# Numbering all transfers in program order over both DMA queues, and storing the last block whole

## The chip, the cores and the metric

The kernel runs on one core of a Trainium2 chip. The metric is device time in microseconds (us). PE is the matrix engine (TensorE), DVE the vector engine, ACT the scalar engine, POOL GpSimd, and SP the sync engine, which computes nothing here and issues transfers. "SPq" and "ACTq" are the instruction queues of SP and ACT when they issue transfers (DMAs). A transfer is asynchronous: the engine issues it, goes on, and a completion semaphore is raised when the data has landed.

## What is computed

q, k and v are float32; S1, S2 and the weights are float64 and reach the device as raw 64-bit words; the output is float32. A sketched attention is followed by a multiplicative feed-forward network:

```python
def phi(x):                                   # 64 features per row
    a = einsum('rd,bhsd->bhsr', S1, x);  b = einsum('rd,bhsd->bhsr', S2, x)
    return (a[..., :, None] * b[..., None, :]).reshape(..., r * r)
q_p, k_p = phi(q), phi(k)                     # q, k, v: batch 4, heads 4, seq 1088, dim 32; r = 8
kv = einsum('bhsf,bhsd->bhfd', k_p, v);  z = k_p.sum(axis=2)
x = (q_p @ kv) / (q_p @ z + 1e-6)             # then to (4352 tokens, 128)
a, b = x @ w1, x @ w2                         # 128 -> 1024
out = ((a * b) @ w3) @ w_out                  # 1024 -> 1024 -> 128
```

## The kernel before

The program is made of some hundreds of named steps. A list written out by hand, `ORDER`, gives the one order in which they are recorded; each step issues its instructions on whichever engines it uses. A helper at the end of the kernel (lines 1544 to 1548) then ties every instruction to the one before it *on the same engine*, so that the scheduler keeps the written order engine by engine. Nothing ties an instruction of one engine to one of another, except data.

The tokens come in eight main groups, `g0` to `g7`, of 512 tokens (two for each batch), and one group `gr` of 256 tokens, the last 64 rows of each of the four batches. For each group the feed-forward part (function `ffn`) runs over eight chunks c of the hidden width: step `a` (line 1458) and step `b` (line 1468) are matmuls, step `c` copies one result out on ACT, step `m` multiplies on DVE, and step `o` (line 1481, for `gr` line 1488) accumulates the product with the folded w3 and w_out into the output bank. w3 and w_out are folded into one matrix earlier, so two matmul layers become one.

At the end of a main group, `g.oT` (line 1497) transposes the output bank into SBUF on DVE, and `g.st` stores it with four DMAs of 64 KB on SP (function `main_dst`, line 1435). These pieces are 128 bytes long at the output (32 floats). The last group `gr` is different. It has two output banks; `gr.oT0` copies bank 0 out on ACT and `gr.oT1` copies bank 1 out on DVE (both line 1508). The stores (function `rest_dst`, line 1441) have pieces of 512 bytes:

- `gr.st0` stores bank 0 whole, 64 KB, from ACT's queue;
- `gr.st1` stores the first half of bank 1, 32 KB, from SP's queue;
- `gr.st2` stores the second half of bank 1, 32 KB, from ACT's queue.

In `ORDER` the tail reads `... g7.oT ... g7.st ... gr.oT0 gr.oT1 gr.st2 gr.st1 gr.st0`, followed by idle matmuls (`warm`). So on SP the four DMAs of `g7.st` come before `gr.st1`, and on ACT `gr.st2` comes before `gr.st0`. Earlier stores on SP, in this order, are those of `g4`, `g5`, `g6`, `g1` and `g2`.

The framework gives the transfers eight completion semaphores in turn, numbered 0 to 7, in the order in which its scheduler takes them. A transfer waits, on the queue that issues it, until the transfer that had its semaphore before has landed. The issuing queue is in order, so everything behind a waiting transfer on that queue waits too. Which transfer gets which number follows from the order that the scheduler took across engines, which the chains of line 1544 leave open.

Loads of inputs and weights are on SP as well, except that the two large loads of the first k block (`k0.load0`, `k0.load1`, line 506) are on ACT. They and the last stores are the only transfers that ACT issues.

Of the kernel before, what the change touches and what calls it, by code (L numbers as in the profile page):

```python
# [112 lines left out]
g4.7o g7.1m g4.oT g6.5m gr.2b g7.4a g6.2b gr.2a g7.4c g7.7a gr.2c gr.2m gr.0b gr.6m g6.2m g7.4m gr.3c g4.st g5.st  # L113
g7.7c g6.0o g6.5o g6.2o g6.6o g6.4o g6.1o g6.3o g6.7o gr.0m g6.oT g7.7b g6.st g7.0o gr.0o0 g7.6o g7.5o gr.3b g1.st
gr.1b g7.4o g2.st g7.2o gr.1m g7.7m gr.3m g7.3o g7.1o g7.7o gr.0o1 gr.6o1 gr.6o0 gr.5o0 g7.oT gr.1o0 gr.5o1 gr.1o1
gr.4o1 gr.3o1 gr.2o1 g7.st gr.7o1 gr.4o0 gr.3o0 gr.2o0 gr.7o0 gr.oT0 gr.oT1 gr.st2 gr.st1 gr.st0 warm25 warm20 warm28
"""


# [4 lines left out]
def make_steps(ctx, tc, q, k, v, S1, S2, moe_w1, moe_w2, moe_w3, moe_w_out, out):  # L124
    nc = tc.nc
    dve, act, pe, pool, sp = nc.vector, nc.scalar, nc.tensor, nc.gpsimd, nc.sync
    B, H, S, D = q.shape
    r = S1.shape[0]
    DM, DF = moe_w1.shape
# [6 lines left out]
    NT = S // 32  # L136
# [6 lines left out]
    def step(name):  # L143
        def keep(f):
            assert name not in steps, name
            steps[name] = f
            return f
        return keep
# [13 lines left out]
    def sb(tag, shape, dtype=F32, bufs=1, name=None):  # L162
        return place(work, tag, shape, dtype, bufs, name or tag)

    def ps(tag, shape, name):
        return place(psum, tag, shape, F32, 1, name)
# [1270 lines left out]
                             oT[i * 32:(i + 1) * 32, :nT * 32].rearrange("p (T d) -> p T d", d=32))  # L1437
        return dst

    def rest_dst(oT, u, t0=0, n=32):  # L1440
        (sp if u and not t0 else act).dma_start(bass.AP(tensor=out.tensor, offset=(NT - 2 + u + t0 * NT) * DM,
                             ap=[[NT * DM, n], [S * DM, B], [1, DM]]), oT[t0 * B:(t0 + n) * B])

    ab_sb, o_ps = {}, {}

    def ffn(g, n, dst):
        for c in range(NC):
            halves = 2 if (g, c) in HALVES else 1
            w = n // halves
            for u in range(halves):  # L1450
                x = {}
                su = "" if halves == 1 else "ab"[u]
                c0 = u * w

                @step(f"g{g}.{c}{su}a")
                def _(c=c, c0=c0, x=x, w=w):
                    x["a"] = ps("h", [128, 512], "a_ps")
                    pe.matmul(x["a"][:, :w], w_of(0, c), xT[g][:, c0:c0 + w], start=True, stop=True)  # L1458

                @step(f"g{g}.{c}{su}c")  # L1460
                def _(x=x, w=w):
                    x["s"] = sb("ffa", [128, 512], bufs=2)
                    act.copy(x["s"][:, :w], x["a"][:, :w])  # L1463

                @step(f"g{g}.{c}{su}b")
                def _(c=c, c0=c0, x=x, w=w):
                    x["b"] = ps("h", [128, 512], "b_ps")
                    pe.matmul(x["b"][:, :w], w_of(1, c), xT[g][:, c0:c0 + w], start=True, stop=True)  # L1468

                @step(f"g{g}.{c}{su}m")  # L1470
                def _(c=c, c0=c0, x=x, u=u, w=w):
                    if u == 0:
                        ab_sb[g, c] = sb("ab", [128, 512])
                    dve.tensor_mul(ab_sb[g, c][:, c0:c0 + w], x["s"][:, :w], x["b"][:, :w])  # L1474

            if g != "r":
                @step(f"g{g}.{c}o")
                def _(c=c):
                    if c == 0:
                        o_ps[g] = ps("out", [128, 512], "ps_o")  # L1480
                    pe.matmul(o_ps[g], w3o[:, c], ab_sb[g, c], start=c == 0, stop=c == NC - 1)  # L1481
            else:
                for u in range(2):
                    @step(f"g{g}.{c}o{u}")
                    def _(c=c, u=u):
                        if c == 0:
                            o_ps[g, u] = ps(("out", "kvz")[u], [128, DM], "ps_or")
                        pe.matmul(o_ps[g, u], ab_sb[g, c][:, u * DM:(u + 1) * DM], w3o[:, c],  # L1488
                                  start=c == 0, stop=c == NC - 1)

        if g != "r":
            oT = {}

            @step(f"g{g}.oT")
            def _():
                oT[0] = sb("oT", [128, 512], bufs=2)
                dve.transpose(oT[0], o_ps[g])  # L1497

            step(f"g{g}.st")(lambda: dst(oT[0]))
        else:  # L1500
            z = {}
            for u in range(2):
                @step(f"g{g}.oT{u}")
                def _(u=u):
                    if u == 0:
                        z["o"] = sb("oT", [128, 512], bufs=2)
                    z[u] = z["o"][:, u * DM:(u + 1) * DM]
                    (dve.tensor_copy if u else act.copy)(z[u], o_ps[g, u])

                if u == 0:  # L1510
                    step(f"g{g}.st0")(lambda: dst(z[0], 0))
                else:
                    for i in range(2):
                        step(f"g{g}.st{1 + i}")(lambda i=i: dst(z[1], 1, 16 * i, 16))

    for g in range(8):
        b, half = divmod(g, 2)
        if g < 2:
            q_part(g, b, half * 512, 512, "AL"[g])
        elif b < 2:  # L1520
            q_wide(g, b, half * 512, 512, lambda t, g=g: (g, t * 128))
        elif half == 0:
            q_wide(g, b, 0, 1024, lambda t, g=g: (g + t // 2, t % 2 * 256))
        ffn(g, 512, main_dst(b, half * 16, 16))
    q_wide("r", None, 0, 256, lambda t: ("r", t))
    ffn("r", 256, rest_dst)

    for i, n in enumerate(WARM):
# [4 lines left out]
@with_exitstack  # L1533
def kernel(ctx: ExitStack, tc: tile.TileContext, *args: bass.AP):
    nc = tc.nc
    steps = make_steps(ctx, tc, *args)
    traced = nc.cur_bb.bb.instructions
    behind = mybir.DependencyInfo(mybir.DependencyClass.NoSync, mybir.DependencyReason.SCHED_ONLY)
    chained = [e.engine for e in (nc.vector, nc.scalar, nc.tensor, nc.gpsimd, nc.sync)]
    last, seen = {}, len(traced)  # L1540
    for name in ORDER.split():
        steps.pop(name)()
    assert not steps, sorted(steps)
    for ins in traced[seen:]:
        if ins.engine in chained:
            if ins.engine in last:
                tc.add_manual_dep(ins, last[ins.engine].name, behind, reason="order")
            last[ins.engine] = ins


# [28 lines left out]
```

## Time and profile before

| what | us |
|---|---|
| median of 3 runs | 256.16 (255.90 to 256.43) |
| the profiled execution, its own time | 255.97 |
| its span in the trace | 254.2 |
| PE busy in it | 245.7 (97%) |
| DVE, ACT, POOL busy | 159.2, 100.3, 82.3 |
| last matmul group of `gr` (line 1488) ends | 247.6 |
| last transfer issued (SP, line 1441) | 251.32 |

The span goes from the first to the last recorded event of the program; the own time of the execution includes what lies around it. The transfers by queue, the first thing that the page says of them, are these (queue and kind, packets, MB, share of the time of 16 DMA engines):

```profile
q1 hardware_dynamic: 30352, 21.02, 33.4%
q10 hardware_dynamic: 768, 0.62, 0.8%
```

q1 is SP's queue and q10 is ACT's. A row of the timeline reads: start in us, length in us, engine, line, operation, output and input, how many, and in brackets the idle time of the engine before it and what ended it. For a transfer the length is that of its issue, not of the data's way; the landing comes later.

### The profile page before, as it was taken

What the parts mean: (1) busy time and instruction counts of PE and PEld (TensorE: products, weight loads), DVE (VectorE), ACT (ScalarE), POOL (GpSimd) and SP (SyncE); (2) the same over time, 40 slices, a digit from 0 to 9 for tenths busy, and PEclk for the clock granted to TensorE, in tenths of its full rate; (3) what the DMA queues carried; (4) which work ended last, traced back from release to release, by engine and by line L of the source; (5) the groups of instructions that cost most, each with busy time, mean ns of one, the idle gap of its engine ahead of it and who ended that gap; (6) DMA issues with size and microseconds to landing.
All of it is one profiled execution on the core that took longest, in us unless ns stands there. A gap on an engine that the chain in (4) does not pass through costs nothing.

```text
span 254.2 us, 6032 instructions
## 1 busy us (share of the span) xinstructions
PE 245.7 (97%) x2511; PEld 140.1 (55%) x2511; DVE 159.2 (63%) x351; ACT 100.3 (39%) x186; POOL 82.3 (32%) x111
## 2 busy tenths in 40 slices
PE   8899999999999999999999999999999999999990
PEld 6789756456644657576454444444435544554570
DVE  4899898999999969647839584523073144531310
ACT  3757689865665675111522343123202200120000
POOL 3269469476273497983002340000000000000000
PEclk9999999999999999999999999999999999999997
DMA  5679856899599420030200000000020000022532
GB/s 184 182 208 361 251 139 155 228 232 235 144 276 232 92 83 0 3 92 1 41 3 3 0 0 5 0 0 3 0 41 0 3 0 0 0 46 37 83 54 52
DMA packets 31147, 22.02 MB, mean 87 GB/s; under 512 B 21264, under 2 KB 25616, under 8 KB 30992
## 3 DMA queue, kind: packets, MB, share of 16 engines
q1 hardware_dynamic: 30352, 21.02, 33.4%
q10 hardware_dynamic: 768, 0.62, 0.8%
q8 instruction: 20, 0.33, 0.6%
q14 instruction: 7, 0.06, 0.1%
HBM read 19.40 MB, written 2.23 MB: 85 GB/s over the span
## 4 chain that ended last, share of the span: by engine, by line
PE 87%; DVE 5%; DMA 2%; POOL 2%; issue 1%; SPq 1%; DVEq 0%; POOLq 0%
PE a_ps L1458 23%; PE b_ps L1468 23%; PE ps_o L1481 22%; PE ps_w3o L480 6%; PE ps_x L1417 2%; PE ps_g L608 2%; PE ps_ac L1303 2%; DMA qh<-in_q_dram 2%; PE ps_or L1488 1%; PE ps_kv L718 1%; POOL RC L345 1%; PE idle_ps L223 1%; PE ps_ab L676 1%; DVE k_m L182 1%; PE ps_kq L754 0%
## 5 line engine op out<-in xcount | busy, mean ns | idle before, releaser
L1474 DVE TENSOR_TENSOR ab<-ffa,b_ps 128x512 f32<-128x512 f32 (+1 forms) x74 | 45.9, 636 | 44.2 <-PE b_ps L1468 34.7
L1463 ACT COPY ffa<-a_ps 128x512 f32<-128x512 f32 (+1 forms) x74 | 38.6, 556 | 86.6 <-PE a_ps L1458 80.8
L1468 PE MATMUL b_ps<-xT,w 128*128 128x512 f32 (+1 forms) x148 | 67.4, 560 | 0.0
L1458 PE MATMUL a_ps<-xT,w 128*128 128x512 f32 (+1 forms) x148 | 66.8, 561 | 0.0
L1481 PE MATMUL ps_o<-ab,w3o 128*128 128x512 f32 x128 | 60.8, 595 | 0.0
L1468 PEld LDWEIGHTS b_ps<-xT,w 128*128 128x128 f32 x148 | 27.4, 190 | 27.9 <-issue 23.4
L1458 PEld LDWEIGHTS a_ps<-xT,w 128*128 128x128 f32 x148 | 27.1, 190 | 27.6 <-issue 22.1
L1481 PEld LDWEIGHTS ps_o<-ab,w3o 128*128 128x128 f32 x128 | 23.8, 190 | 26.0 <-issue 24.3
L444 POOL TENSOR_TENSOR w3c<-cv_c,cv_m 128x512 int32<-128x512 int32 x16 | 20.3, 1284 | 12.5 <-DVE cv_c L433 8.8
L1497 DVE STREAM_TRANSPOSE oT<-ps_o 128x512 f32<-128x512 f32 x8 | 5.7, 713 | 18.7 <-PE ps_o L1481 18.7
L480 PEld LDWEIGHTS ps_w3o<-wo,w3T 128*128 128x128 f32 x128 | 15.4, 192 | 2.9 <-issue 2.2
L480 PE MATMUL ps_w3o<-wo,w3T 128*128 128x128 f32 x128 | 15.4, 275 | 0.0
L1350 POOL TENSOR_TENSOR s_hl<-s_hl,ay_C 128x256 f32<-128x256 f32 (+2 forms) x4 | 3.2, 794 | 37.1 <-DVE s_hl L1346 25.8
L223 PE MATMUL idle_ps<-zeros 128*128 128x256 bf16 x72 | 12.8, 312 | 1.0 <-DVE zeros L195 1.0
L419 ACT ACTIVATE cv_m<-raw 128x1024 int32<-128x1024 uint32 x11 | 13.0, 1183 | 0.0
L231 ACT ACTIVATE cv_c<-raw 128x1024 f32<-128x1024 f32 x11 | 12.8, 1173 | 0.2 <-DMA raw<-in_moe_w_dram 0.2
L626 POOL TENSOR_TENSOR kp<-kabt 128x1024 f32<-128x1024 f32 x6 | 12.1, 2028 | 1.9 <-DVE kabt L694 1.2
L474 DVE STREAM_TRANSPOSE w3T<-w3c 128x1024 f32<-128x1024 f32 x8 | 9.8, 1224 | 1.0 <-POOL w3c L444 1.0
L223 PEld LDWEIGHTS <-zeros 128*128 128x128 bf16 x72 | 7.7, 110 | 4.0 <-issue 1.3
L1398 POOL TENSOR_TENSOR ph<-s_al,s_bs 128x1024 f32<-128x1024 f32 x2 | 5.1, 2560 | 9.2 <-DVE s_bs L1388 9.2
L1428 ACT COPY xT<-ps_x 128x128 f32<-128x128 f32 (+2 forms) x20 | 4.7, 324 | 8.6 <-PE ps_x L1417 8.6
L608 PE MATMUL ps_g<-kk 128*32 128x64 f32 x288 | 7.8, 224 | 0.3 <-DVE kk L600 0.3
(245 smaller groups left out, 302.5 us busy)
## 6 DMA issues: line engine op xcount, KB each, us to landing
raw<-in_moe_w_dram SPq DMA_DIRECT2D x32, 256.0 KB, 6.2
qh<-in_q_dram SPq DMA_DIRECT2D x4, 544.0 KB, 6.0
raw<-in_moe_w_dram SPq DMA_DIRECT2D x4, 512.0 KB, 7.1
out_dram<-oT SPq DMA_DIRECT2D x32, 64.0 KB, 2.0
k<-in_k_dram SPq DMA_DIRECT2D x3, 512.0 KB, 4.0
v<-in_v_dram SPq DMA_DIRECT2D x2, 512.0 KB, 6.4
raw<-in_moe_w_out_dram SPq DMA_DIRECT2D x1, 1024.0 KB, 8.1
kh<-in_k_dram SPq DMA_DIRECT2D x8, 128.0 KB, 2.5
```

What stands on the lines that cost most here:

```text
L223: pe.matmul(t, zeros, bview(zeros, [[0, 2], [1, 128]]), start=True, stop=True)
L231: act.activation(dst, hi.bitcast(F32), ACT.Prelu, scale=2.0 ** -112, alpha=-2.0 ** 32)
L419: act.mul(x["m"], words(0).bitcast(U32), 2.0 ** -29)
L444: pool.tensor_tensor(d, c, m, ALU.add)
L480: pe.matmul(t["o"], w3T[ko][:, c], wo[:, c], start=c == 0, stop=c == NC - 1)
L608: pe.matmul(o[h * D:(h + 1) * D], lhs, rhs, start=start, stop=stop, skip_group_check=True)
L626: eng.tensor_mul(dst, bview(av, [list(av.ap[1]), list(av.ap[2]), [0, r]]), bview(bv, [list(bv.ap[1]), [0, r], list(bv.ap[2])]))
L1458: pe.matmul(x["a"][:, :w], w_of(0, c), xT[g][:, c0:c0 + w], start=True, stop=True)
L1463: act.copy(x["s"][:, :w], x["a"][:, :w])
L1468: pe.matmul(x["b"][:, :w], w_of(1, c), xT[g][:, c0:c0 + w], start=True, stop=True)
L1474: dve.tensor_mul(ab_sb[g, c][:, c0:c0 + w], x["s"][:, :w], x["b"][:, :w])
L1481: pe.matmul(o_ps[g], w3o[:, c], ab_sb[g, c], start=c == 0, stop=c == NC - 1)
```

## The change

Three edits:

1. In the closing loop, every transfer (an instruction of the class `InstDMACopy`) also gets an ordering edge to the transfer before it in program order, whichever queue issues it. The edge is of the kind that only orders the schedule (`NoSync`), as are the chains by engine that were there before.
2. `rest_dst` loses its parameters for parts; it stores a whole bank, bank 0 from ACT, bank 1 from SP.
3. The steps `gr.st1` and `gr.st2` become one, `gr.st1`, of 64 KB; the list loses the word `gr.st2`.

```diff
-gr.4o1 gr.3o1 gr.2o1 g7.st gr.7o1 gr.4o0 gr.3o0 gr.2o0 gr.7o0 gr.oT0 gr.oT1 gr.st2 gr.st1 gr.st0 warm25 warm20 warm28
+gr.4o1 gr.3o1 gr.2o1 g7.st gr.7o1 gr.4o0 gr.3o0 gr.2o0 gr.7o0 gr.oT0 gr.oT1 gr.st1 gr.st0 warm25 warm20 warm28
...
-    def rest_dst(oT, u, t0=0, n=32):
-        (sp if u and not t0 else act).dma_start(bass.AP(tensor=out.tensor, offset=(NT - 2 + u + t0 * NT) * DM,
-                             ap=[[NT * DM, n], [S * DM, B], [1, DM]]), oT[t0 * B:(t0 + n) * B])
+    def rest_dst(oT, u):
+        (act, sp)[u].dma_start(bass.AP(tensor=out.tensor, offset=(NT - 2 + u) * DM,
+                                       ap=[[NT * DM, 32], [S * DM, B], [1, DM]]), oT)
...
-                if u == 0:
-                    step(f"g{g}.st0")(lambda: dst(z[0], 0))
-                else:
-                    for i in range(2):
-                        step(f"g{g}.st{1 + i}")(lambda i=i: dst(z[1], 1, 16 * i, 16))
+                step(f"g{g}.st{u}")(lambda u=u: dst(z[u], u))
...
             last[ins.engine] = ins
+        if isinstance(ins, mybir.InstDMACopy):
+            if "dma" in last:
+                tc.add_manual_dep(ins, last["dma"].name, behind, reason="order")
+            last["dma"] = ins
```

## The prediction

> **What bounds the kernel now.** I read the page's busy shares first: PE is busy 97% of a 254.2 us span, so a change to transfers can pay only where PE has stopped or waits. The chain of work that ended last, asked for the stretch from 240 us on, says where it has stopped (start us, length us, what):
>
> ```profile
> 239.97 4.29 PE ps_o L1481 x10
> 244.26 3.35 PE ps_or L1488 x30
> 247.60 0.33 PE idle_ps L223 x3
> ```
>
> The chain ends with idle matmuls at 247.93, yet the span is 254.2: the last 6.3 us hold no compute at all. The waits of the sync queue (SPq) from 240 us on (total us, times, longest us) tell what they hold:
>
> ```profile
> SPq L1435 <- DMA out_dram<-oT: 4.7, 2, 4.2
> SPq L1435 <- DVE oT L1497: 2.4, 1, 2.4
> SPq L1574 <- DMA out_dram<-oT: 1.1, 1, 1.1
> SPq L1574 <- PEq L1574: 0.6, 2, 0.4
> ```
>
> The first row is the stall: stores of line 1435 (the `g7.st` step) waited 4.7 us for other *stores* to land, not for data. The third is the final wait for the last transfer. The timeline of the tail, in narrow windows, shows each issue alone:
>
> ```profile
> 244.29 0.72 DVE L1497 STREAM_TRANSPOSE oT<-ps_o 128x512 f32<-128x512 f32 x1 [2.94 <-PE ps_o L1481]
> 245.04 0.32 SPq L1435 DMA_DIRECT2D out_dram<-oT  x1
> 246.75 0.29 DVE L1508 COPY oT<-ps_or 128x128 f32<-128x128 f32 x1 [1.74 <-PE ps_or L1488]
> 247.64 0.27 ACT L1508 COPY oT<-ps_or 128x128 f32<-128x128 f32 x1 [18.48 <-PE ps_or L1488]
> 247.70 0.63 ACTq L1441 DMA_DIRECT2D out_dram<-oT  x1
> 248.43 0.58 ACTq L1441 DMA_DIRECT2D out_dram<-oT  x1
> 249.61 0.32 SPq L1435 DMA_DIRECT2D out_dram<-oT  x1
> 250.38 0.32 SPq L1435 DMA_DIRECT2D out_dram<-oT  x1
> 250.74 0.49 SPq L1435 DMA_DIRECT2D out_dram<-oT  x1
> 251.32 0.61 SPq L1441 DMA_DIRECT2D out_dram<-oT  x1
> ```
>
> The data of `g7.st` is ready at 245.01 and its first quarter leaves at 245.04; the second leaves only at 249.61. In the built program the transfers take eight completion semaphores in turn, and each transfer waits until the one before it on its semaphore has landed. There the two ACT stores (`gr.st2`, `gr.st0`) hold semaphores 5 and 6 as if they came before `g1.st`'s last quarter, though they run last; the second and third quarters of `g7.st` come round to 5 and 6. So SP waits for `gr.st2`, issued 247.70 and seen landed at 249.61 (1.91 us), then for `gr.st0`, issued 248.43 and seen landed at 250.38 (1.95 us). The last half of the rest, `gr.st1`, stands behind all that on SP and leaves at 251.32. From that issue to the end of the span it is 2.87 us (254.19 - 251.32): the landing and the closing barrier. The end is set by a ring of completion numbers; the data of that last store had been ready since 247.04.
>
> Landing times, from the transfers' rows of the page (x, KB each, us from issue to landing):
>
> ```profile
> out_dram<-oT SPq DMA_DIRECT2D x32, 64.0 KB, 2.0
> out_dram<-oT ACTq DMA_DIRECT2D x1, 64.0 KB, 1.9
> out_dram<-oT SPq DMA_DIRECT2D x1, 32.0 KB, 1.9
> ```
>
> 32 or 64 KB make no difference that these rows show. And how fast SP issues stores that nothing holds up, from a narrow window in the burst of twelve that starts at 236.23:
>
> ```profile
> 237.67 1.05 SPq L1435 DMA_DIRECT2D out_dram<-oT  x2
> ```
>
> Two in 1.05 us, of which one issue alone is 0.50: 0.55 us from one start to the next.
>
> **The change, part by part.** *Renumbering.* In the built program of the changed kernel the quarters of `g7.st` wait for semaphores 2, 3, 4 and 5, whose last users are the four quarters of `g1.st` (5th to 8th of the burst, landed by about 242). So all four leave at once: 245.04, then at the burst's pace about 245.4, 245.95 and 246.5, done by 247.0. This removes the 4.2 and the 0.45 us waits. `gr.st1` now takes semaphore 6 and `gr.st0` semaphore 7; their last users are the first two quarters of `g2.st`, issued about 240.4 and 240.96, landed 2.0 us later, by 243.0. Both are free four us before they are wanted.
>
> *The whole store on sync.* `gr.st1` now carries 64 KB. It waits for the DVE copy, done at 247.04, and for SP's own queue, free at about 247.03: it leaves at about 247.1, lands at 247.1 + 1.95 = 249.05. Not last.
>
> *One store less on ACT.* `gr.st2` is gone, so `gr.st0` no longer waits for its 0.63 us of issue. What it waits for is the ACT copy of `gr.oT0`, 247.64 + 0.27 = 247.91. No row shows ACT's queue wait for ACT's own result; the nearest are DVE to SP (245.01 to 245.04, 0.03 us) and PE to ACT (247.60 to 247.64, 0.04 us). Bounds of its start: 247.94 from below, and from above the 248.43 it has now. I take 247.96, by the nearer rows.
>
> *The sum.* The last issue moves from 251.32 to 247.96: -3.36 us. For the 64 KB landing I add 1.95 - 1.91 = 0.04 us. Net -3.3 us: span 254.2 - 3.3 = 250.9. The profiled execution took 255.97, 1.8 us outside its span, and lies 0.19 below the median of 256.16; carried to the median, 256.16 - 3.3 = **252.85**.
>
> *Edits costed at nothing.* The order edges are between instructions of a schedule; on every engine the built program has the same instructions in the same order but for the one store, so no compute moves. At the start the numbers of the first five transfers swap: SP's load at 5.37 us (`k2.loadr`) now waits for ACT's first load of k, which DVE was already reading at 3.56; cover 1.8 us. If it were gone, `k2.loadr` would be late, but the next on SP is a load that left only at 11.24 for other reasons. In the burst at 236 to 242 five stores now wait for transfers older than before, so never for longer. Each is hidden while PE works until 247.6.
>
> *What contention could add.* In the kernel before, ACT's stores flew alone: the stretch 247 to 248 us shows 0 DMA packets. Now six stores (384 KB) leave within 245.04 to 248.6. The packet windows give the parts of `gr.st0`'s 1.95 us: issue 248.43, packets from 249.65 to 250.0, seen 250.38; that is 1.22 us until the first, 0.35 of data, 0.38 until it is seen. Moved to 247.96, its packets go at 249.2 to 249.55. `gr.st1`'s go at about 248.3 to 248.65 by the same parts. The gap is 0.5 us, so I take 0; if they met in full, one would pass the other its 0.35 us: bounds 0 and +0.35.
>
> The Trainium skill ("DMA: Bandwidth & Descriptors", section on queues, rings and completion order) speaks against this: a completion increment lands only after every earlier write of that DMA engine, across its queues, so `gr.st0` would also wait for SP's small-piece stores. By that rule the end is still 252.85 as long as `gr.st1` lands before 249.9; no row of this trace shows two store queues in flight together.
>
> **The rivals.**
>
> *B, the last stores meet.* SP's four stores of 128-byte pieces run slower next to the others, or ACT's wait for its own copy is long. For: in the burst the DMA engines were 70 to 78% busy (3-us windows), so little is spare. Against: landing stayed 2.0 us in it. Price: +0.35 for data met in full, or up to +0.47 for the start at 248.43: 253.2 to 253.7.
>
> *C, the numbers don't matter and only the store count does.* If the ring stayed, `gr.st0` (247.96, landing 249.9) would release the second quarter at 249.9, the rest following at 250.3, 250.8 and `gr.st1` at 251.35, against 251.32 now: 256.2, no change. Against: the built program's waits, named above.
>
> *D, on the other side: the chain across queues acts as a wait for landing.* Then each transfer would wait for the one before it, on whichever queue. From 245.04: four quarters at 1.95 us, `gr.st1` at 252.8, `gr.st0` at 254.8, end 254.8 + 2.9 = 257.7 against 254.2: 3.5 us slower, 259.7, the loads not counted. It decides as soon as one store's issue waits for the last but one. Against: the built program has no such waits; SP's store waits stand eight transfers apart.
>
> *E, another wait takes half.* The closing barrier or ACT's end of queue turns out late once SP is early. For: four engines' closing drains are not on the chain shown. Against: ACT's drain starts at 249.1 and takes 0.4, and moves up with its queue. About 254.5.
>
> **How the numbers follow.** Forecast 0.80 (252.4 to 253.2), B 0.10 (253.2 to 253.7), E 0.04, C 0.03, D 0.03. The predicted time is the forecast's, 252.85. The range goes from 252.85 less the 0.3 that runs of before spread round their median, and 0.1 for a landing at its shortest row (1.8), 252.4, to B's end, 253.7; that leaves out about one in ten. About 0.2% (0.5 us) is what a measurement of this kernel can tell from no change. Faster by more: forecast, B and E, 0.94. Same: C, 0.03. Slower: D, 0.03.
>
> **What would show it.** Right: no row of line 1435 waiting for out_dram; four L1435 issues within 245.0 to 247.0; SP's L1441 near 247.1 and ACT's near 247.96; the wait of SP's line 1574 for out_dram grown from 1.1 to about 2.1 us, since SP is done earlier than the last landing; compute rows unmoved. Wrong: ACT's L1441 later than 248.2 or landing over 2.3 us (B); a gap left between L1435's issues (C); two stores a landing apart (D); more than 1.1 us from the last landing to the span's end (E).

## The result and the profile after

The changed kernel took 253.05 us (median of 4 runs, 252.73 to 253.67) against 256.03 us before (median of 4): ratio 0.9885, 95% interval 0.9861 to 0.9908. Forecast was 252.85 with a range of 252.4 to 253.7. The span fell from 254.2 to 251.2 us. Some executions of these kernels run about 2% longer at a lower granted clock (the one trace of the last variant below: a span of 256.2 us at a clock of 0.973); the ratios and medians leave them out.

The waits of the sync queue from 240 us on, in the changed kernel:

```profile
SPq L1435 <- DVE oT L1497: 2.4, 1, 2.4
SPq L1574 <- DMA out_dram<-oT: 1.8, 3, 0.7
SPq L1574 <- PEq L1574: 0.6, 2, 0.4
```

The row in which line 1435 waited 4.7 us for other stores is gone; the wait for data (DVE) is as it was. SP's closing wait for landings grew from 1.1 to 1.8 us, because SP is now done before the last store lands.

The timeline of the tail in the changed kernel (rows of compute that don't matter here left out):

```profile
244.68 0.72 DVE L1497 STREAM_TRANSPOSE oT<-ps_o 128x512 f32<-128x512 f32 x1 [2.94 <-PE ps_o L1481]
245.43 2.04 SPq L1435 DMA_DIRECT2D out_dram<-oT  x4
247.14 0.29 DVE L1508 COPY oT<-ps_or 128x128 f32<-128x128 f32 x1 [1.74 <-PE ps_or L1488]
247.57 0.62 SPq L1441 DMA_DIRECT2D out_dram<-oT  x1
...
248.03 0.27 ACT L1508 COPY oT<-ps_or 128x128 f32<-128x128 f32 x1 [18.49 <-PE ps_or L1488]
248.33 0.64 ACTq L1441 DMA_DIRECT2D out_dram<-oT  x1
```

From the start of the first issue to the end of the last, the four quarters of `g7.st` take 2.04 us, where they took 6.19 us before (245.04 to 251.23). SP's whole store follows at 247.57. The last issue is ACT's, at 248.33, which is 0.03 us after the copy it waits for ends (248.03 + 0.27). The path to the end is now the one of data: PE, copy, store, landing, closing barrier.

The last pieces of the chain that ended last, in the same kernel, show where the rest of the difference to the forecast sits:

```profile
240.35 4.29 PE ps_o L1481 x10
244.65 3.35 PE ps_or L1488 x30
247.99 0.33 PE idle_ps L223 x3
```

The matmuls take exactly as long as before (4.29 and 3.35 us), but the last group ends at 247.99 instead of 247.60. This execution was 0.39 us late at PE already, and the tail was shortened by more than the span shows. A measure that this lateness can't touch is the time from the start of ACT's last copy to the end of the span: 254.2 - 247.64 = 6.56 us before, 251.2 - 248.03 = 3.17 us after, 3.4 us less. The experiments are read by it beside their medians.

### The profile page after: what moved, and what is told of

The parts are those of the page before. It is cut to its first block, busy times and chain, and to the rows that moved or that the text cites. A ratio compares the mean times of both kernels' runs of the same rounds, so it can differ in the third digit from the quotient of the medians.

```text
span 251.2 us, 6030 instructions
## 1 busy us (share of the span) xinstructions
PE 245.5 (98%) x2511; PEld 139.6 (56%) x2511; DVE 159.0 (63%) x351; ACT 100.1 (40%) x186; POOL 82.6 (33%) x111
## 4 chain that ended last, share of the span: by engine, by line
PE 92%; DVE 3%; DMA 2%; SPq 1%; issue 1%
PE a_ps L1458 24%; PE b_ps L1468 23%; PE ps_o L1481 22%; PE ps_w3o L480 6%; PE ps_g L608 3%; PE ps_x L1417 2%; PE ps_ac L1303 2%; DMA kr<-in_k_dram 2%; PE ps_kv L718 2%; PE ps_or L1488 1%; PE idle_ps L223 1%; PE ps_xt L1199 1%; PE ps_ab L676 1%; DVE k_m L182 1%; PE ps_kq L754 0%
## 5 line engine op out<-in xcount | busy, mean ns | idle before, releaser
L1406 DVE STREAM_TRANSPOSE pT<-ph 128x1024 f32<-128x1024 f32 (+1 forms) x7 | 7.8, 1141 | 0.0
```

## The experiments

Two theories stood against each other. **Numbering**: the gain is the vanished wait on the ring of completion semaphores, plus 0.4 to 0.5 us for ACT's single store. **One store less**: the gain comes from the merged store and the edges do nothing. Beside them, three small questions: where the 0.39 us came from, whether ACT's queue is needed, and what it costs when stores meet.

The numbers of all runs (medians over the executions that the ratios use):

| kernel | median us | ratio to before, 95% interval | ACT's last copy to the end of the span, us |
|---|---|---|---|
| before | 256.03 to 256.18 | 1 | 6.6 |
| changed | 253.05 | 0.9885 (0.9861 to 0.9908) | 3.2 |
| changed, again | 252.79 | 0.9876 (0.9852 to 0.9899) | 250.9 - 247.74 = 3.2 |
| edges alone | 253.26 | 0.9905 (0.9876 to 0.9935) | 251.4 - 247.66 = 3.7 |
| merged store alone | 255.56 | 0.9970 (0.9951 to 0.9989) | 253.8 - 247.71 = 6.1 |
| both stores on SP, no edges | 252.76 | 0.9865 (0.9848 to 0.9882) | 250.7 - 247.61 = 3.1 |
| the same, again | 252.59 | 0.9866 (0.9849 to 0.9882) | 250.8 - 247.74 = 3.1 |
| the same, k transpose later | 252.54 | 0.9864 (0.9847 to 0.9880) | no comparable trace |
| changed, stores made to meet | 254.06 | 0.9924 (0.9904 to 0.9944) | 252.1 - 247.47 = 4.6 |

### The changed kernel again

No edit.

> The changed kernel again, to have it beside the others and to size the gain. Both theories: near 253.0 us, 2.9 to 3.3 below the kernel before. If the 0.39 us by which PE ended later in its first trace is chance, its matmuls end anywhere from 247.5 to 248.5 over runs and the median gain stays near 3.0; the last issue follows PE's end by about 0.35 us (0.04 to the copy, 0.27 of copy, 0.03 to the issue).

Measured: 252.79 us, ratio 0.9876; PE's last matmul group ended at 247.71, ACT's copy started at 247.74 and its store at 248.04. The last issue follows PE's end by 0.33 us, as expected, and PE's end moved by 0.28 us between two traces of one and the same kernel. That is the size of the difference between the two medians (253.05 and 252.79); with one trace of each it is a likeness, and not shown to be the cause.

### The edges alone

```diff
             last[ins.engine] = ins
+        if isinstance(ins, mybir.InstDMACopy):
+            if "dma" in last:
+                tc.add_manual_dep(ins, last["dma"].name, behind, reason="order")
+            last["dma"] = ins
```

The three stores of the last group stay as in the kernel before.

> The order edges between all transfers alone; three stores as before, two of them from ACT. Theory 'numbering': no wait of line 1435 for out_dram is left, the four quarters of g7.st leave within 2.1 us, and the end is set by ACT's second store, held 0.45 to 0.5 us by the issue of the first (0.63 us from 0.06 after the copy's start): 0.4 to 0.5 us slower than the changed kernel, so 2.5 to 2.9 us below before, 253.2 to 253.6. Rival 'one store less': the gain comes from the merged store, and with three stores the time is that of before, 256.0.

Measured: 253.26 us. SP's waits have no row of line 1435 for out_dram, and the tail of the timeline reads:

```profile
245.06 2.04 SPq L1435 DMA_DIRECT2D out_dram<-oT  x4
247.19 0.61 SPq L1441 DMA_DIRECT2D out_dram<-oT  x1
...
247.66 0.27 ACT L1508 COPY oT<-ps_or 128x128 f32<-128x128 f32 x1 [18.49 <-PE ps_or L1488]
247.72 1.32 ACTq L1441 DMA_DIRECT2D out_dram<-oT  x2
```

Here SP is done early, as in the changed kernel; what is left over is ACT, where the second store has to wait for the issue of the first. It leaves at 248.45, 0.79 us after the copy's start, against 0.30 us in the changed kernel: 0.49 us, about the difference of the medians beside the repeat (253.26 - 252.79 = 0.47). The intervals of these two ratios overlap, so the size rests on the traces. The edges alone bring 2.8 of the 3.4 us. "One store less" as the source of the whole gain has fallen.

### The merged store alone

```diff
         if ins.engine in chained:
             ...
             last[ins.engine] = ins
-        if isinstance(ins, mybir.InstDMACopy):
-            if "dma" in last:
-                tc.add_manual_dep(ins, last["dma"].name, behind, reason="order")
-            last["dma"] = ins
```

This is the changed kernel without its edges.

> The merged store alone, no edges across queues. In the built program ACT's store then has semaphore 5 and stands before the last quarters of g1.st; the third quarter of g7.st comes round to it. Theory 'numbering': two quarters leave at once, the third waits until ACT's store has landed (PE's end + 0.35 + 1.95), the fourth and gr.st1 follow 0.36 and 0.9 us later; the last issue is 0.4 to 0.5 us earlier than before's: 255.5 to 255.7, and line 1435 waits for out_dram once, about 4 us. Rival 'one store less': the whole gain, 253.0.

Measured: 255.56 us, in the middle of what "numbering" gave. The waits of SP from 240 us on:

```profile
SPq L1435 <- DMA out_dram<-oT: 4.0, 1, 4.0
SPq L1435 <- DVE oT L1497: 2.4, 1, 2.4
```

And the timeline's tail, from windows around each issue:

```profile
245.11 0.32 SPq L1435 DMA_DIRECT2D out_dram<-oT  x1
245.47 0.49 SPq L1435 DMA_DIRECT2D out_dram<-oT  x1
...
248.01 0.64 ACTq L1441 DMA_DIRECT2D out_dram<-oT  x1
...
250.01 0.85 SPq L1435 DMA_DIRECT2D out_dram<-oT  x2
250.96 0.62 SPq L1441 DMA_DIRECT2D out_dram<-oT  x1
```

Two quarters leave at once. The third goes at 250.01, which is ACT's issue plus its landing (248.01 + 2.0). The data of the third quarter had lain ready since 245.1, and the first of the two rows on the waits names a store's landing as what ended this one. One store in the ring instead of two shortens the stall from 4.7 to 4.0 us and the tail by 0.5 us. So the merge by itself saves little; with the ring mended it saves 0.47 us, the issue on ACT. By the stretch from ACT's copy to the end the parts add up, 2.8 for the edges and 0.5 for the merge against 3.4 for both, but the 0.5 is saved at two different places: in SP's queue while the ring is wrong, in ACT's once it is mended.

### Both stores on SP, without edges

```diff
     def rest_dst(oT, u):
-        (act, sp)[u].dma_start(bass.AP(tensor=out.tensor, offset=(NT - 2 + u) * DM,
+        sp.dma_start(bass.AP(tensor=out.tensor, offset=(NT - 2 + u) * DM,
                                        ap=[[NT * DM, 32], [S * DM, B], [1, DM]]), oT)
```

and the edges left out as in the run above.

> No edges across queues; both stores of the last group from SP, so that ACT has no transfer but the two first loads and the numbers at the end follow SP's own order; the numbers of the first five transfers are those of before. Theory 'numbering': the same as the changed kernel within 0.2 us, 253.0, since SP is free when ACT's copy is done, and its store then leaves 0.03 to 0.06 us after the copy. Rival 'ACT's queue is needed' (two queues side by side make the tail short): 0.6 us or more slower. Rival 'early numbers': if the swapped numbers at the start made PE 0.39 us late in the changed kernel, this one is 0.4 us faster, 252.65.

Measured: 252.76 us, and 252.59 in the repeat below. SP's waits have no row of line 1435 for out_dram here either, and its issues read:

```profile
245.00 2.10 SPq L1435 DMA_DIRECT2D out_dram<-oT  x4
247.20 1.29 SPq L1441 DMA_DIRECT2D out_dram<-oT  x2
```

The second of the last two leaves at 247.91, 0.04 us after ACT's copy is done (247.61 + 0.27). With one queue at the end there is nothing to misnumber, and the numbers at the start are those of the kernel before. The time is that of the changed kernel within the intervals. So neither is ACT's queue needed, nor did the swapped numbers at the start cost 0.39 us: with them undone the repeat of the changed kernel is matched (252.79 and 252.76).

### The stores made to meet

```diff
-gr.4o1 gr.3o1 gr.2o1 g7.st gr.7o1 gr.4o0 gr.3o0 gr.2o0 gr.7o0 gr.oT0 gr.oT1 gr.st1 gr.st0 warm25 warm20 warm28
+gr.4o1 gr.3o1 gr.2o1 gr.7o1 gr.4o0 gr.3o0 gr.2o0 gr.7o0 gr.oT0 gr.oT1 gr.st1 g7.st gr.st0 warm25 warm20 warm28
```

> The changed kernel with the step g7.st put behind gr.st1 in the order, so that SP's four stores of small pieces are in flight while ACT's last store is. SP: gr.st1 near 247.2, the quarters of g7.st at about 247.8, 248.4, 248.9 and 249.4, the last landing 2.0 us later, at 251.4; end 252.3, so about 1.4 us slower than the changed kernel: 254.2. ACT's store leaves at 248.0. Theory 'stores share without harm' (the forecast's zero for contention): it lands within 2.1 us, as alone. Rival 'the last stores meet' and the rule that a completion waits for earlier writes across queues: its landing grows by 0.35 us or more, to 2.3 to 2.9 us; the time then still follows SP's last store, which may land late too.

Measured: 254.06 us, as worked out. The longer time is that of SP's last quarter, which now leaves only at 249.28 and lands 2.0 us later; ACT's store lands before it and is not on the path. So the price of meeting is read from landings, not from the time. Now ACT's store flies among SP's. The transfers from 246 us on (KB each, median us from issue to landing), first of the changed kernel:

```profile
out_dram<-oT SPq DMA_DIRECT2D x4, 64.0 KB, 2.0
out_dram<-oT ACTq DMA_DIRECT2D x1, 64.0 KB, 2.0
```

then of this one:

```profile
out_dram<-oT SPq DMA_DIRECT2D x5, 64.0 KB, 2.1
out_dram<-oT ACTq DMA_DIRECT2D x1, 64.0 KB, 2.2
```

and its windows (us, busy PE, PEld, DVE, ACT, POOL, granted clock, share of the DMA engines, GB/s), with the engines nearly full while the two queues overlap:

```profile
248.00:249.00 1.00, 0.00 (x0) 0.00 (x0) 0.00 (x0) 0.00 (x0) 0.00 (x0) 1.00 0.47 105
249.00:250.00 1.00, 0.00 (x0) 0.00 (x0) 0.00 (x0) 0.00 (x0) 0.00 (x0) 1.00 0.92 166
```

ACT's store landed after 2.2 us instead of 2.0, and SP's first quarter, issued 0.2 us before it, after 2.3 us. Neither theory has it quite: meeting costs 0.2 to 0.3 us of landing, more than nothing and less than the 0.35 of full overlap. In the changed kernel the packets of the last two stores don't meet (SP's run from 248.84 to 249.20, ACT's from 249.62 to 249.98) and both stores land in 2.0 us, so the zero taken there stands. The Trainium skill ("DMA: Bandwidth & Descriptors", queues, rings and completion order) says that a completion waits for earlier writes of the same DMA engine across queues. Here ACT's store, issued at 247.77, landed at about 250.0, and SP's earlier quarter, issued at 247.56, at about 249.8. The order agrees with the rule, but plain sharing of busy engines would give it too. What the trace adds is where the price lies: ACT's packets took 0.54 us (249.12 to 249.67) instead of 0.36 in the changed kernel, and from the last of them to the landing it was 0.34 us in both. Most of the 0.2 us is in the data, and this run shows no further wait behind it.

### The transpose of the small k load moved back

```diff
-k0.lead1 q0.tr kr0.tr s.rest warm18 k0.rest0 s.T s.tc
+k0.lead1 q0.tr s.rest warm18 k0.rest0 s.T kr0.tr s.tc
```

on top of both stores on SP, with three entries of the slot list turned so that every step keeps its PSUM slot.

> Both last stores from SP, no edges across queues, and at the start PE's transpose of the small k load (kr0.tr, line 768) moved behind the transposes of line 308, with the PSUM slots of the three steps kept. If the 0.39 us of lateness in the changed kernel's first trace is this transpose waiting for its load (PE waited 0.99 us for it there, 0.41 and 0.28 us in two other traces, not at all in three), PE no longer waits there: PE's end at 247.5 to 247.7 in every run, the time the same or up to 0.2 us below that of both stores on SP, and the runs closer together. If the lateness comes from elsewhere, no change.

> Both last stores from SP, no edges across queues, again: 252.76 within 0.2 us, the base for the run beside it.

Measured: ratio 0.9864 with the step moved and 0.9866 without, on the same chip. No gain, and no narrower spread that these few runs could show. What the traces do show is a wait that comes and goes. PE's waits in the first 12 us of the changed kernel's first trace:

```profile
PE idle_ps L223 <- DVE zeros L195: 1.0, 1, 1.0
PE ps_krt L768 <- DMA kr<-in_k_dram: 1.0, 1, 1.0
```

The second row is not there in the kernel before, and it is 0.4 us in the repeat of the changed kernel. It also stands, with 0.3 us, in the trace of the edges alone and, with 0.5 us, in the repeat of both stores on SP, which has no edges; so it doesn't go with the edges. What PE waits for is the second half of the load, issued at 3.59 us in the kernel before and in the changed one. It landed after 4.0 us before and after 5.0 us in the first trace of the changed kernel, while the first half took 4.5 us in both. In that trace the chain that ended last runs through it:

```profile
3.59 5.04 DMA kr<-in_k_dram
8.77 0.30 PE ps_krt L768
```

SP's load of line 506, which waits for PE, leaves at 11.71 us there and at 11.24 before, so the lateness is there by then. In the three traces with the shorter waits it leaves at 11.26 to 11.35. That this landing made PE 0.39 us late in the first trace is therefore well supported. Moving the step did not make the kernel faster, and no comparable trace of the moved step is there to show whether its wait went. Why the landing varies stays open.

## Why the prediction was right

**The reading of the tail** held. The 4.2 us stall was the ring's; it went away with the numbering and came back, 4.0 us long, when the edges were taken out with all else kept.

**The burst of four quarters** was given as starts 0, 0.36, 0.9 and 1.45 us after the first, and came as 0, 0.36, 1.0 and 1.54. SP's whole store was given at 0.05 us after the DVE copy's end (247.1 in that forecast's time), and left 0.14 us after it (247.57 against 247.43); SP's queue had been busy with the fourth quarter until 247.47. Neither is on the path.

**ACT's store** was given 0.05 us after the copy, between 0.03 and 0.52; it came 0.03 us after it. Its landing was given as 1.95 us and took 2.0. These are the terms that set the sum.

**The sum**: -3.3 us. By the stretch from ACT's copy to the end it was -3.4 in both traces of the changed kernel. By the medians it was 3.0 (256.03 - 253.05) in the first set and 3.4 (256.18 - 252.79) in the second. What the sum lacked is a term for PE's end: I took it as fixed at 247.6, and over the eight comparable traces, of kernels whose matmuls are the same, it lies anywhere from 247.44 to 247.99. That the medians 253.05 and 252.79 come so close to 252.85 is therefore in part luck; what the runs confirm is the shorter tail, to 0.1 us.

**Edits at nothing**: the numbers at the start were priced at nothing with 1.8 us of cover. `k2.loadr` left at 5.38 us in the changed kernel and at 5.37 before, and the run without the swap agrees.

**The rivals.** B (the last stores meet) did not happen in the changed kernel; made to happen, it cost 0.2 to 0.3 us of landing, somewhat under its price of 0.35; no run has it on the path to the end. One reading of the trace before was too strong: from 249.61 to 250.38 ACT's `gr.st0` and SP's second quarter were both between issue and landing, and only their packets never overlapped (249.67 to 250.03 and from 250.45 on). C (the ring stays) was tried as the merged store alone: it gave 255.56 and not the 256.2 of the forecast, because the scheduler then puts ACT's one store on semaphore 5 and only the last two quarters of `g7.st` queue up behind it. I had kept the ring as it was, with the second quarter waiting. D (edges act as waits) has fallen: the four quarters leave 0.36 to 0.64 us apart, not a landing apart. E (a late closing barrier) did not come: from the last issue to the end it was 251.2 - 248.33 = 2.9 us, as before (254.2 - 251.32). One sign was off by its measure: SP's closing wait was to grow to 2.1 us and the row says 1.8. From the end of SP's last issue to ACT's landing it was 2.1 us (248.19 to 250.33), but the wait is now split among several landings, and the time between its parts is not in the row.

## What to carry to other kernels

Where completion semaphores are handed out in turn, as here, a transfer waits not only for its data but for whoever held its number before, and if the numbers follow a scheduler's order instead of the time at which transfers run, an early store can queue behind a late one of another queue. The sign in a profile is a queue that waits for the landing of *stores* while its own data lies ready; the remedies that worked here are edges that only order the schedule, or giving the last transfers to one queue. To size such a change, measure from the last common event (here ACT's copy) to the end, so that lateness from elsewhere doesn't blur it.

## What the runs showed of the hardware

Most of the two microseconds of the last store lie ahead of its data. ACT's store of 64 KB in the kernel before was issued at 248.43, its packets ran from about 249.65 to 250.0, and the waiting queue went on at 250.38: 1.2 us until the first packet, 0.35 of data, 0.4 until the completion was seen. In the changed kernel it was 248.33, 249.6 to 250.0 and a landing at about 250.33. The Trainium skill ("DMA: Bandwidth & Descriptors", in its part on where the fixed two microseconds go) puts most of them on the receipt of the write, in its account of transfers that GpSimd issues. ACT issues these, so the page and the traces don't speak of the same path; here at most 0.4 us lie between the last packet and the landing. I had also not expected the landing of half a small load (`kr`) to move from 4.2 to 5.0 us between two executions of the changed kernel that issue it at the same time (3.60 and 3.59 us).
